# Turning the query tile of twenty middle token tiles with transposing transfers on SyncE's queue instead of fp16 transposes on TensorE

## The chip, the cores and the metric

The kernel runs on one core of a Trainium2 chip. Times are device microseconds (us) of one execution. The engines named here are TensorE (PE in the profile; PEld is its weight load, which overlaps it), VectorE (DVE), ScalarE (ACT), GpSimd (POOL) and SyncE (SP). SP computes nothing: it issues the DMA transfers, one after the other, in the order of its program. Each engine works through its own program strictly in order, and semaphores make one wait for another.

## The reference, cut to what matters

The input is 2048 tokens of 512 values. Four sublayers follow each other: Fourier mixing (A), a mixture of tiny experts (B), and both once more. Everything is computed in 32 bits, with a residual and a layer norm around each.

```python
def _A_ref(x, dft_seq_re, dft_seq_im, dft_hid_re, dft_hid_im):
    a = jnp.einsum("bsd,ed->bse", x, dft_hid_re)
    b = jnp.einsum("bsd,ed->bse", x, dft_hid_im)
    return jnp.einsum("ts,bse->bte", dft_seq_re, a) - jnp.einsum("ts,bse->bte", dft_seq_im, b)

def _B_ref(x, w_q, k1, k2, u, v):          # H = 32 heads, E = 16 keys a side, K = 2
    ...
    s1 = jnp.einsum("nhd,ed->nhe", q1, k1)
    s2 = jnp.einsum("nhd,ed->nhe", q2, k2)
    i1 = jnp.argsort(-s1, axis=-1)[..., :K]
    i2 = jnp.argsort(-s2, axis=-1)[..., :K]
    ...
    g = _softmax(top_s, axis=-1)          # top_s, top_e: the best 2 of the 4 sums, and their experts
    act = _gelu(jnp.einsum("nd,nhkd->nhk", xf, u[top_e]))
    return jnp.einsum("nhk,nhk,nhkd->nd", g, act, v[top_e])

x = x + _A_ref(_layernorm(x), ...)
x = x + _B_ref(_layernorm(x), ...)
x = x + _A_ref(_layernorm(x), ...)
x = x + _B_ref(_layernorm(x), ...)
```

## The kernel before

**Two layers of two stages.** Each layer (A and then B) is cut into nine units of the sequence: seven of 256 tokens and two of 128. For a unit, the sequence stage (`seq_unit`) multiplies the normalised input, kept whole in SBUF as a high part `xh`/`xg` and a low part `xl`/`xm`, by the columns of the sequence DFT. Those columns are streamed: a 256 KB piece is loaded into `raw` (line 454, four buffers), split by ACT into `ch` (line 458, three buffers) and by DVE into `cl` (line 462), and used by twelve matmuls of 512 columns (line 518), which add up in PSUM (`acc`). One piece is used up, and one is loaded, about every 2.7 us of pure sequence work.

**The token tiles.** When a unit is done, each of its tiles of 128 tokens goes through `token_tile`: the hidden DFT (line 668), residual, layer norm, a turn of the normalised tile, scores against the 2 x 16 keys of each of the 32 heads (lines 784 and 788), and products with the 256 experts (line 818). ACT evacuates the scores (line 793). DVE then searches the best two keys a side (lines 880 to 912) and builds `q`, three slices of 128 x 128 fp16: the first key's number, the second's, and the softmax weights. Line 985 writes the last of the keys and line 1007 the last of the weights. There are 32 tiles in all, 16 a layer.

**From `q` to the expert weights.** `q` has a token on each partition and must be turned. `f_pq` does it with three fp16 transposes on PE (line 1018), which read `q` as stationary operand and write the PSUM tile `pq`; it takes one of the four `bank` buffers for that. ACT copies `pq` to `qt` in another order of elements (`f_qt`, line 1022). DVE compares `qt` with a table of numbers (line 1041, four instructions of 1024 columns) and multiplies by the weights (line 1047, two), into `lr`. PE multiplies these in 32 small matmuls (`f_blocks`, line 1057), ACT evacuates them (line 1089), SP writes them to DRAM (line 1116, `gdr`) and reads them back in another order (line 1124, `gt`), and DVE multiplies the activations by them (line 1131). Most tiles of the second layer are put off after that: their last product is done at the end (`off`).

**What sets the order.** Every step is an `Op` of a planner (`Plan.run`) with an engine, a planned duration, the steps it waits for, and the buffers it takes and gives back. The planner simulates the engines by a list of costs and, at each point, takes for an engine the step that can start first, ties by priority. The instructions are then written out by planned start, so that each engine has one fixed order. A DMA step has a duration on SP, a `lag` until its data are there and a `shy` as margin. Work of the sequence stage has the lowest priority on PE: it fills the time in which tiles wait for other engines. While a tile is searched, PE works on the next unit's sequence stage, and DVE interleaves the search of one tile with the comparisons of another and with the `cl` of the pieces.

A third kind of transfer matters as a comparison: in most tiles the normalised tile is turned through DRAM. DVE turns its 32 x 32 blocks, SP writes them out (line 726, `xdr`) and reads them back in four transfers of 64 KB (line 735, `tok`).

Of the kernel before, what the change touches and what calls it, by code (L numbers as in the profile page):

```python
# [11 lines left out]
F16 = mybir.dt.float16  # L12
# [4 lines left out]
P = 128  # L17
# [7 lines left out]
SP = 1  # L25
# [13 lines left out]

def MOVED(layer, at):  # L40
    return at >= 2 if layer == 0 else at < NCH + NSC * (TPC - 1) - 2


def DEFERRED(layer, at):
# [33 lines left out]
class Plan:  # L78
# [10 lines left out]
    def op(self, engine, us, fn, after=(), take=(), last=(), prio=(0, 0), lag=0.0, behind=(), shy=0.0):  # L89
        o = Op(len(self.ops), engine, us, fn, [a for a in after if a is not None], list(take), list(last), prio, lag,  # L90
               list(behind), shy)
        for h in o.last:
            h.users += 1
        self.ops.append(o)
        return o
# [60 lines left out]
MM512, MM256, TR32, TR16, MMG = 0.230, 0.121, 0.110, 0.057, 0.026  # L156
# [6 lines left out]
def act(n):  # L163
    return 0.09 + n / 1.2e3
# [7 lines left out]
def spectral_peer_kernel(ctx: ExitStack, tc, x_in, cseq, ctile, dhid, wq, k1t, k2t, ut, vm, out):  # L172
    nc = tc.nc
# [6 lines left out]


    BUFS = {"acc": 4, "bank": 4, "raw": 4, "c": 3, "p": 1, "row": 4, "wr": 5, "wp": 2,
            "tok": 3, "sc": 1, "eq": 1, "act": 3, "q": 2, "top": 1, "qt": 1, "lr": 4, "gt": 1, "pp": 1, "gdr": 2, "xdr": 2, "bn": 1, "pick": 1}
    plan = Plan(BUFS)


# [41 lines left out]
    def work(shape, dtype, name, pool=None):  # L228
        return work_pool().tile(shape, dtype, name=name, bufs=BUFS[pool or name])
# [7 lines left out]
    op = plan.op  # L237
# [368 lines left out]
    last = {}  # L606
# [3 lines left out]
    def token_tile(layer, n, i, t0, at):  # L610

        prio = (0, layer, at if at < len(units) - 1 else -1 - layer, i)
# [5 lines left out]
        t = {}  # L618
# [6 lines left out]
        a = None  # L625
# [31 lines left out]
        for cs in wide:  # L657
            hb, nc_ = Hold("bank"), cs.stop - cs.start
            for z, (k, ms) in enumerate(steps):
                def f(z=z, k=k, ms=ms, cs=cs):  # L660
# [4 lines left out]
                    for c in range(2):  # L665
# [6 lines left out]
                a = op("PE", 2 * len(ms) * (MM512 if nc_ == D else MM256), f, [pready[layer, n][k][2 in ms], a] + dft_done + seed,  # L672
                       take=[hb] if z == 0 and not fine else [], behind=[a_row],
                       last=[phold[layer, n]] if z == len(steps) - 1 else [], prio=prio)
# [11 lines left out]
        if fine:  # L686
            a = ln_rest(lambda: t["bn"].rearrange("p a b -> p (a b)"), hbn, i, bn_done, prio)
        else:
            a = ln_stats(lambda: t["row"], i, [b] + ([xready[1, i]] if (1, i) in xready else []), prio)
# [60 lines left out]
        for z, k in enumerate([] if moved else ks):  # L750
# [16 lines left out]
            hb = Hold("bank")  # L767
            a = op("PE", (k.stop - k.start) * TR32, f_tr, [xn[z]], take=[hb], last=[hx], prio=prio)
# [7 lines left out]
        for hf in range(2):  # L776
            hb = Hold("bank")
# [21 lines left out]
            if fine:  # L799
                for z, k in enumerate(ks):  # L800
                    a_pe = op("PE", 2 * (k.stop - k.start) * MM512, lambda f=f_pch, hf=hf, k=k: f(hf, k), [a_th[z], a_pe],
                              take=[] if z else [hb], prio=prio)
# [8 lines left out]
        hb, hact, hg = Hold("bank"), Hold("act"), Hold("act")  # L811
# [13 lines left out]
        a = op("PE", 12 * MM256, f_xu, [a_pe], take=[hb], last=[hth, htl], prio=prio)  # L825
        a = op("ACT", act(N), f_act, [a], take=[hact], last=[hb], prio=late)
# [6 lines left out]
        a = op("ACT", act(N), f_g0, [a], take=[hg], prio=late)  # L833
        a = op("ACT", act(N), lambda: nc.scalar.activation(t["g0"], t["g0"], AF.Copy, bias=1.0), [a], prio=late)
        a = op("DVE", dve(N), lambda: nc.vector.tensor_mul(t["g0"], t["g0"], t["act"]), [a], prio=late)
        a = op("ACT", act(N), lambda: nc.scalar.activation(t["g0"], t["g0"], AF.Tanh, scale=C0), [a], prio=late)
        a = op("ACT", act(N), lambda: nc.scalar.activation(t["g0"], t["g0"], AF.Copy, bias=1.0), [a], prio=late)
# [3 lines left out]
        heq, hq, htop = Hold("eq"), Hold("q"), Hold("top")  # L841
# [91 lines left out]
        if fine:  # L933
            left, a_val, a_key, first = [], [], [], []
            for f in range(2):
                part = slice(f, f + 1), slice(f * H, (f + 1) * H), 32
                order_ = prio + (f,)
                a = largest(0, *part[1:], lambda f=f: t["pc", f], scored[f:f + 1], order_, **hold, behind=first)
# [5 lines left out]
                a = eq(0, *part[1:], view, a, order_)  # L944
                a = code(0, *part, a, order_)
                left += without(*part, view, a, order_, last=banks[f:f + 1], take=[] if f else [hsc])
                hold = {}
                a = tree32(1, *part[1:], left[f:], order_)
                a_val += a
                a = eq(1, *part[1:], lambda c=part[1]: flat("sc")[:, :, c], a, order_, last=[hsc])  # L950
                a_key += code(1, *part, a, order_)
        else:
            a = tree32(0, cols, w, sc_parts, prio, **hold)
            a = eq(0, cols, w, lambda: flat("sc"), a, prio)
            a = code(0, fs, cols, w, a, prio)
            a = without(fs, cols, w, lambda: flat("sc"), a, prio)
            a_val = tree32(1, cols, w, a, prio)
            a = eq(1, cols, w, lambda: flat("sc"), a_val, prio, last=[hsc])
# [48 lines left out]
        c5 = op("DVE", 0.13, lambda: nc.vector.tensor_sub(t["q"][:, 2, :, 1], t["gw"], t["q"][:, 2, :, 0]), [c4], last=[htop], prio=prio)  # L1007
# [14 lines left out]
            nc.scalar.copy(t["qt"].rearrange("p r (q j) -> p r q j", q=16),  # L1022
                           t["pq"].rearrange("p r (j q) -> p r q j", q=16))

        a = op("PE", 3 * TR16 + 0.06, f_pq, [c5, d2], take=[hb], last=[hq], prio=prio)
        a_qt = op("ACT", act(384), f_qt, [a], take=[hqt], last=[hb], prio=prio)

        def row_of(r, hf):
            m = t["qt"][:, r].rearrange("p (a b) -> p a b", b=4)[:, 16 * hf:16 * hf + 16]
# [79 lines left out]
        moves, back = [], []  # L1109
# [8 lines left out]
        for j in range(0 if fine else 2):  # L1118
            def f_in(j=j):
                if j == 0:  # L1120
                    t["gt"] = work([P, E, E], F32, "gt")
                d = t["gdr"][j]
                d = bass.AP(d.tensor, d.offset, [[STEP, 64], [4 * ROW, E], [1, E]])
                nc.sync.dma_start(t["gt"][j * 64:(j + 1) * 64], d)
# [220 lines left out]
```

## Time and profile before

| | us |
|---|---|
| median of 3 runs | 1233.59 (1233.14 to 1234.08) |
| the profiled execution, whole | 1233.48 |
| its span, first to last instruction | 1231.7 |
| DVE busy | 1000.1 |
| ACT busy | 492.2 |

Busy time is the time in which an engine runs at least one instruction. The instructions of PE overlap: a matmul of 512 columns is shown with some 390 ns, and the next one starts 0.23 us after it, so that what an instruction costs PE is the distance between two starts and not its duration. The same holds on DVE, where an instruction's shown duration reaches some 0.09 us into the next one.

### The profile page before, as it was taken

How to read it: one execution, taken by the hardware profiler on the slowest of the kernel's cores; microseconds unless marked ns; L12 is line 12 of the kernel's file. 1: busy time of each engine (PE TensorE's matmuls, PEld its weight loads, DVE VectorE, ACT ScalarE, POOL GpSimd, SP SyncE). 2: the span in 40 equal slices, each digit the busy share in tenths (PEclk: the TensorE clock that was granted, in tenths of full speed). 3: DMA queues.
4: the chain of work that ended last, by engine and by line, in shares of the span. 5: the costliest groups of instructions: out<-in, count | busy, mean ns of one | idle time of the engine just before them, and what ended most of it. 6: DMA issues, size and time to landing. Idle time of an engine off the chain costs nothing. (4 is left out here: it accounts for less than half of the span.)

```text
span 1231.7 us, 20733 instructions
## 1 busy us (share of the span) xinstructions
PE 1220.1 (99%) x7626; PEld 1014.5 (82%) x7626; DVE 1000.1 (81%) x2272; ACT 492.2 (40%) x1010; POOL 45.0 (4%) x71
## 2 busy tenths in 40 slices
PE   9999999999999999999999999999999999999998
PEld 6877778878788888899988988788888888888886
DVE  8899997999897785968987359959596786859796
ACT  7522234334343333324654233334343333343455
POOL 2000000000000000000000000000000000000000
PEclk9999999999999999999999999999999999999999
DMA  7866551453444244441656243563635254454464
GB/s 241 261 200 218 188 169 35 101 119 83 123 122 113 70 116 116 107 120 49 172 142 174 79 120 82 125 135 92 154 97 140 73 145 111 99 141 104 115 204 144
DMA packets 312726, 160.12 MB, mean 130 GB/s; under 512 B 216752, under 2 KB 283056, under 8 KB 312624
## 3 DMA queue, kind: packets, MB, share of 16 engines
q1 hardware_dynamic: 312480, 158.66, 48.2%
q8 instruction: 60, 0.98, 0.3%
q14 instruction: 42, 0.34, 0.1%
q10 hardware_dynamic: 144, 0.13, 0.0%
HBM read 120.73 MB, written 38.01 MB: 129 GB/s over the span
## 5 line engine op out<-in xcount | busy, mean ns | idle before, releaser
L518 PE MATMUL acc<-ch,xh 128*128 128x512 f32 (+1 forms) x868 | 328.3, 378 | 0.8 <-DVE ptl L547 0.8
L518 PE MATMUL acc<-cl,xh 128*128 128x512 f32 (+1 forms) x868 | 321.9, 371 | 0.0
L518 PE MATMUL acc<-ch,xl 128*128 128x512 f32 (+1 forms) x868 | 321.7, 371 | 0.0
L458 ACT CAST ch<-raw 128x512 fp32r<-128x512 f32 x256 | 158.6, 620 | 272.0 <-PE acc L518 222.7
L462 DVE TENSOR_TENSOR cl<-raw,ch 128x512 fp32r<-128x512 f32 x256 | 176.0, 688 | 61.6 <-ACT ch L458 51.4
L518 PEld LDWEIGHTS acc<-cl,xh 128*128 128x128 f32 x868 | 163.6, 188 | 28.8
L518 PEld LDWEIGHTS acc<-ch,xh 128*128 128x128 f32 x868 | 163.6, 189 | 28.0 <-issue 1.8
L518 PEld LDWEIGHTS acc<-ch,xl 128*128 128x128 f32 x868 | 163.8, 189 | 25.6
L880 DVE TENSOR_TENSOR tmp<-sc 128x512 f32<-128x512 f32 (+1 forms) x64 | 43.5, 680 | 72.9 <-ACT sc L793 72.6
L784 PE MATMUL bank<-wh,tok 128*128 128x512 f32 x256 | 100.3, 392 | 0.3 <-ACT tok L742 0.3
L784 PE MATMUL bank<-wl,tok 128*128 128x512 f32 x256 | 99.7, 389 | 0.0
L668 PE MATMUL bank<-dh,pth 128*128 128x512 f32 x248 | 98.6, 397 | 0.0
L668 PE MATMUL bank<-dl,pth 128*128 128x512 f32 x248 | 96.7, 390 | 0.0
L668 PE MATMUL bank<-dh,ptl 128*128 128x512 f32 x248 | 93.6, 390 | 0.0
L793 ACT COPY sc<-bank 128x512 f32<-128x512 f32 x62 | 36.1, 588 | 138.1 <-PE bank L788 108.0
L1041 DVE TENSOR_TENSOR lr<-iota,qt 128x1024 f16<-128x1024 f16 x124 | 81.0, 686 | 12.0 <-ACT qt L1022 11.9
L260 POOL TENSOR_TENSOR stats<-stats,half 128x1 f32<-128x1 f32 x64 | 43.7, 689 | 1149.1 <-DVE stats L257 1135.1
L867 DVE TENSOR_TENSOR eq<-sc,val 128x1024 f16<-128x1024 f32 (+1 forms) x64 | 77.2, 1207 | 1.5
L518 PE MATMUL acc<-ch,xg 128*128 128x512 f32 (+1 forms) x204 | 77.3, 379 | 0.0
L518 PE MATMUL acc<-cl,xg 128*128 128x512 f32 (+1 forms) x204 | 75.7, 371 | 0.0
L518 PE MATMUL acc<-ch,xm 128*128 128x512 f32 (+1 forms) x204 | 75.7, 371 | 0.0
L788 PE MATMUL bank<-wh,tok 128*128 128x512 f32 x256 | 68.4, 389 | 0.0
(190 smaller groups left out, 2057.8 us busy)
## 6 DMA issues: line engine op xcount, KB each, us to landing
raw<-in_cseq SPq DMA_DIRECT2D x224, 256.0 KB, 2.8
wr<-in_wq SPq DMA_DIRECT2D x32, 512.0 KB, 3.8
gdr<-lr SPq DMA_DIRECT2D x62, 256.0 KB, 3.7
raw<-in_ctile SPq DMA_DIRECT2D x32, 256.0 KB, 2.9
xdr<-lr SPq DMA_DIRECT2D x25, 256.0 KB, 2.8
tok<-xdr SPq DMA_DIRECT2D x100, 64.0 KB, 2.6
wr<-in_x SPq DMA_DIRECT2D x16, 256.0 KB, 3.3
row<-in_x SPq DMA_DIRECT2D x16, 256.0 KB, 4.0
```

Source lines behind the costliest of these rows:

```text
L260: nc.gpsimd.tensor_tensor(st[:, 1:2], st[:, 1:2], half, op=ALU.pow)
L458: nc.scalar.copy(t[1], t[0])
L462: nc.vector.tensor_sub(t[2], t[0], as32(t[1]))
L518: nc.tensor.matmul(target(d), w[s][:, d * P:(d + 1) * P], moving(s % per, part), start=(s == 0 and k == 0 and d % blocks == 0), stop=(s == ...
L668: nc.tensor.matmul(t["y", cs.start], w[:, k, c, t0:t0 + P], r[:, c, k, cs], start=(not fine and z == 0 and c == 0 and m == 0), stop=(z == ...
L784: nc.tensor.matmul(t["pc", hf], t["th"][:, k, :], r[:, k, hf], start=(k == 0 and r is wh), stop=False)
L788: nc.tensor.matmul(t["pc", hf], t["tl"][:, k, :], wh[:, k, hf], start=False, stop=(k == KD - 1))
L793: nc.scalar.copy(t["sc"][:, :, hf, :], t["pc", hf].rearrange("p h e -> p e h"))
L867: nc.vector.tensor_tensor(t["eq"][:, :, cols], scores(), val(rank_, cols), op=ALU.is_equal)
L880: nc.vector.tensor_max(t["tmp"][:, :, cols], flat("sc")[:, :8, cols], flat("sc")[:, 8:, cols])
L1041: nc.vector.tensor_tensor(t["m", hf, r], io2, row_of(r, hf), op=ALU.is_equal)
```

## The change

For the tiles of units 2 to 6 in the order of each layer (two tiles each, so ten tiles a layer and twenty in all), the three transposes on PE go. In their place SP issues three transfers with `transpose=True`, each of one 128 x 128 fp16 slice of `q`, from SBUF to SBUF, into a new buffer `qi`. The first two wait for the keys (`d2`), the third for the weights (`c5`). The ACT copy to `qt` stays and reads `qi` in place of the PSUM tile. The planner is given 0.5 us on SP for each, a lag of 3.0 and a margin of 0.5 us, and it makes a new order for all engines.

```diff
+def Q_MOVED(layer, at):
+    return 2 <= at < 7
...
-            "tok": 3, "sc": 1, "eq": 1, "act": 3, "q": 2, "top": 1, "qt": 1, "lr": 4, "gt": 1, "pp": 1, "gdr": 2, "xdr": 2, "bn": 1, "pick": 1}
+            "tok": 3, "sc": 1, "eq": 1, "act": 3, "q": 2, "top": 1, "qt": 1, "lr": 4, "gt": 1, "pp": 1, "gdr": 2, "xdr": 2, "qi": 1, "bn": 1, "pick": 1}
...
-        a = op("PE", 3 * TR16 + 0.06, f_pq, [c5, d2], take=[hb], last=[hq], prio=prio)
-        a_qt = op("ACT", act(384), f_qt, [a], take=[hqt], last=[hb], prio=prio)
+        if Q_MOVED(layer, at):
+            hqi, back = Hold("qi"), []
+            for r in range(3):
+                def f_in(r=r):
+                    if r == 0:
+                        t["pq"] = work([P, 3, P], F16, "qi")
+                    nc.sync.dma_start(t["pq"][:, r, :], t["q"][:, r].rearrange("p k a h -> p (k a h)"), transpose=True)
+                back.append(op("SP", 0.5, f_in, [(c5, d2)[r < 2]], behind=back[-1:], take=[] if r else [hqi], last=[hq], prio=prio, lag=3.0, shy=0.5))
+            a_qt = op("ACT", act(384) + 0.05, f_qt, back, take=[hqt], last=[hqi], prio=prio)
+        else:
+            a = op("PE", 3 * TR16 + 0.06, f_pq, [c5, d2], take=[hb], last=[hq], prio=prio)
+            a_qt = op("ACT", act(384), f_qt, [a], take=[hqt], last=[hb], prio=prio)
```

Three places of the new order follow, all around the first tile of the fifth unit of the first layer, a moved one. Line numbers of the change are 4 higher up to the diff's last piece and 14 higher behind it. The first place is PE, where this tile's products with the experts (line 818, in the change 822) end. Before:

```order
L818 MATMUL bank<-ul,tok 128x256
L818 MATMUL bank<-uh,tok 128x256
L1018 LDWEIGHTS q
L1018 MATMUL bank<-ident_109,q 128x128
L1018 LDWEIGHTS q
L1018 MATMUL bank<-ident_109,q 128x128
L1018 LDWEIGHTS q
L1018 MATMUL bank<-ident_109,q 128x128
L518 MATMUL acc<-ch,xh 128x512
L518 MATMUL acc<-ch,xl 128x512
```

And of the change:

```order
L822 MATMUL bank<-ul,tok 128x256
L822 MATMUL bank<-uh,tok 128x256
L522 MATMUL acc<-ch,xh 128x512
L522 MATMUL acc<-ch,xl 128x512
L522 MATMUL acc<-cl,xh 128x512
```

The transposes are gone. Between the last row of line 818 and the first of line 1057 (of the change, 822 and 1071) PE has 30 matmuls of 512 columns of the sequence stage before, and 45 in the change: the small products of this tile stand 15 matmuls later.

The second place is DVE, from the end of the same tile's `q` to its first comparisons with `qt` (line 1041, in the change 1055); `tmp`, `val` and `eq` belong to the search of the unit's other tile. Before:

```order
L985 TENSOR_TENSOR q<-key,df 128x2x64
L1007 TENSOR_TENSOR q<-gw,q 128x2x32
L880 TENSOR_TENSOR tmp<-sc 128x512
L887 TENSOR_TENSOR tmp<-tmp 128x256
L887 TENSOR_TENSOR tmp<-tmp 128x128
L887 TENSOR_TENSOR val<-tmp 128x64
L1041 TENSOR_TENSOR lr<-iota,qt 128x1024
L462 TENSOR_TENSOR cl<-raw,ch 128x512
L1041 TENSOR_TENSOR lr<-iota,qt 128x1024 x2
```

And of the change:

```order
L1011 TENSOR_TENSOR q<-gw,q 128x2x32
L884 TENSOR_TENSOR tmp<-sc 128x512
L891 TENSOR_TENSOR tmp<-tmp 128x256
L891 TENSOR_TENSOR tmp<-tmp 128x128
L891 TENSOR_TENSOR val<-tmp 128x64
L871 TENSOR_TENSOR eq<-sc,val 128x1024
L466 TENSOR_TENSOR cl<-raw,ch 128x512
L901 TENSOR_TENSOR eq<-eq,iota 128x1024
L839 TENSOR_TENSOR act<-act 128x256
L907 TENSOR_TENSOR eq<-eq 128x512
L466 TENSOR_TENSOR cl<-raw,ch 128x512
L1055 TENSOR_TENSOR lr<-iota,qt 128x1024 x3
```

Six instructions of the other tile and of the pieces have moved ahead of the first comparison.

The third place is SP, from the loads ahead of the same tile's three transfers to the transfers behind them. Before:

```order
L454 DMA raw<-in_cseq 128x2x256 x6
L1116 DMA gdr<-lr 128x8x64 x2
L622 DMA row<-in_x 128x512 x2
L454 DMA raw<-in_cseq 128x2x256
L1124 DMA gt<-gdr 64x16x16 x2
```

And of the change:

```order
L458 DMA raw<-in_cseq 128x2x256 x3
L1035 DMA_TRANSPOSE qi<-q 128x128 x3
L458 DMA raw<-in_cseq 128x2x256 x3
L626 DMA row<-in_x 128x512 x2
L458 DMA raw<-in_cseq 128x2x256
L1130 DMA gdr<-lr 128x8x64 x2
L458 DMA raw<-in_cseq 128x2x256
L1138 DMA gt<-gdr 64x16x16 x2
```

The three transfers stand in the middle of the loads of the sequence pieces, and three such loads are queued right behind them. Over the whole program SP has 60 of these rows, three for each of the twenty tiles.

## The prediction

> **What bounds the kernel now.** I read the page first: the engines' shares, and the clock that PE was granted.
>
> ```profile
> span 1231.7 us, 20733 instructions
> PE 1220.1 (99%) x7626; PEld 1014.5 (82%) x7626; DVE 1000.1 (81%) x2272; ACT 492.2 (40%) x1010; POOL 45.0 (4%) x71
> PEclk9999999999999999999999999999999999999999
> ```
>
> PE is busy for 1220.1 of 1231.7 us at an undisturbed clock. The time by stretches shows whether that holds where the change acts: the moved tiles of the two layers lie inside these two stretches. The columns are the stretch, its length, then busy time and instructions of PE, PEld, DVE, ACT and POOL, then clock, DMA share and GB/s.
>
> ```profile
> 250.00:620.00 370.00, 368.14 (x2233) 310.20 (x2232) 307.27 (x739) 144.22 (x303) 15.98 (x23) 1.00 0.44 110
> 790.00:1160.00 370.00, 369.18 (x2047) 305.18 (x2046) 278.92 (x642) 138.57 (x289) 6.47 (x12) 1.00 0.48 116
> ```
>
> In both, PE idles for under 2 us of 370, and ACT is busy for under 40%. The view of PE's waits (us in total, times, longest) says the same of the place of the change:
>
> ```profile
> PE bank L1162 <- DVE act L1131: 1.2, 2, 0.9
> PE bank L1057 <- ACT lr L1089: 0.7, 1, 0.7
> PE bank L1018 <- DVE q L985: 0.3, 1, 0.3
> ```
>
> So PE's stream of instructions sets the time. Work taken off PE is time gained one for one, as long as no new wait stands in that stream; and a wait in it is time lost one for one, since PE has no idle time in which to catch up.
>
> **What is removed.** The timeline of PE at the first moved tile of the fifth unit (start, duration, instruction):
>
> ```profile
> 428.16 0.28 PE L818 MATMUL bank<-uh,tok 128*128 128x256 f32 x1
> 428.28 0.34 PE L1018 MATMUL bank<-ident,q 128*128 128x128 f16 x3
> 428.43 0.47 PE L518 MATMUL acc<-ch,xh 128*128 128x512 f32 x1
> 428.74 0.39 PE L518 MATMUL acc<-ch,xl 128*128 128x512 f32 x1
> 428.97 0.40 PE L518 MATMUL acc<-cl,xh 128*128 128x512 f32 x1
> ```
>
> Starts count, not durations. From the first transpose to the second matmul behind them PE takes 428.74 - 428.28 = 0.46 us; one of the two steps is a matmul of 512 columns, which takes 428.97 - 428.74 = 0.23. The three transposes thus cost PE 0.23 us and not the 0.66 that three durations would give. Twenty tiles: 20 x 0.23 = **4.6 us**. The 0.3 us of the wait row above is too small to count. The PSUM buffer that is no longer taken releases nothing, since PE waits for no buffer worth naming.
>
> **What is added, and its cover.** Three transfers a tile stand between `q` and ACT's copy. The chain today, for the same tile, from the timelines of DVE, ACT and PE:
>
> ```profile
> 426.62 0.22 DVE L1007 TENSOR_TENSOR q<-gw,q 128x64 f16<-128x64 f32 x1
> 428.74 0.49 ACT L1022 COPY qt<-bank 128x384 f16<-128x384 f16 x1
> 429.32 0.69 DVE L1041 TENSOR_TENSOR lr<-iota,qt 128x1024 f16<-128x1024 f16 x1
> 433.53 0.69 DVE L1047 TENSOR_TENSOR lr<-lr,qt 128x1024 f16<-128x1024 f16 x1
> 435.45 0.69 PE L1057 MATMUL bank<-lr 128*64 128x64 f16 x32
> ```
>
> `q` is whole at 426.62 + 0.22 = 426.84, the copy begins 1.9 us later, DVE compares and multiplies until 434.22, and PE reaches its small products at 435.45, 1.2 us after they could begin. The change gives this chain more room on two engines. On PE the small products stand 15 matmuls later: 15 x 0.23 = 3.4 us, less the 0.23 that PE saves ahead of them, so 3.2. [...] On DVE six instructions stand ahead of the first comparison that stood behind it. Their groups (busy, mean ns of one):
>
> ```profile
> L867 DVE TENSOR_TENSOR eq<-sc,val 128x1024 f16<-128x1024 f32 x62 | 75.9, 1223 | 1.5
> L462 DVE TENSOR_TENSOR cl<-raw,ch 128x512 fp32r<-128x512 f32 x256 | 176.0, 688 | 61.6 <-ACT ch L458 51.4 <-PE acc L518 8.9 <-DMA xdr<-lr 0.9
> L897 DVE TENSOR_TENSOR eq<-eq,iota 128x1024 f16<-128x1024 f16 x62 | 42.5, 686 | 0.1
> L835 DVE TENSOR_TENSOR act<-act 128x256 f32<-128x256 f32 x32 | 13.5, 421 | 0.1
> L903 DVE TENSOR_TENSOR eq<-eq 128x512 f16<-128x512 f16 x62 | 26.2, 422 | 0.1
> ```
>
> With `cl` twice that is 1.22 + 2 x 0.69 + 0.69 + 0.42 + 0.42 = 4.1 us, or 3.6 by distances between starts (each shown duration reaches 0.09 us into the next). DVE thus comes to the comparison at 429.32 + 3.6 = 432.9; taking off the copy's 0.49 and 0.1 for handing over, the transfers must have landed by 432.3, **5.4 us after `q`**. Both engines give about the same room; I take 5.4.
>
> No row of before shows a transposing transfer, so its cost is bounded by other transfers. The plain load of a piece, the turn through DRAM and the reload of `gt`, from the views of their lines (min/median/max ns of the issue on SP), then us from issue to landing of the turn, and two rows of the page's list of issues (us to landing):
>
> ```profile
> L454 SPq DMA_DIRECT2D raw<-in_cseq x224: 367/373/1265, 1.2 to 1109.3; - x112
> L1124 SPq DMA_DIRECT2D gt<-gdr x62: 579/639/738, 226.4 to 1211.5; - x62
> L735 SPq DMA_DIRECT2D tok<-xdr x100: 562/628/845, 268.3 to 1101.6; - x100
> ...
> DMA to landing us min/median/max: 2.2/2.6/3.7
> x2d<-row SPq DMA_DIRECT2D x16, 256.0 KB, 2.0
> raw<-in_cseq SPq DMA_DIRECT2D x224, 256.0 KB, 2.8
> ```
>
> From below: an issue of 0.37 and a landing after 2.0, so the third slice is there 2 x 0.37 + 2.0 = 2.7 us after `q`. From above: the three run wholly one behind another, each as long as the slowest turn, 3 x 3.7 = 11.1 us. These ends are far apart on both sides of 5.4. The nearest row is the turn itself: it too comes in a row of small transfers that put data on other partitions. By it the third slice lands after 2 x 0.63 + 2.6 = **3.9 us**, and after 5.0 with the slowest landing seen. I take 3.9, which fits into 5.4 with 1.5 us to spare; PE then waits for nothing new.
>
> **The other queues.** SP gets 60 x 0.63 = 38 us of issuing, 1.9 us at a time, and in-order waits for `q`. Behind it stand loads of pieces. What they can bear is on the timeline of SP and ACT, and in the group of the cast:
>
> ```profile
> 430.63 0.37 SPq L454 DMA_DIRECT2D raw<-in_cseq  x1
> ...
> 431.93 0.62 ACT L458 CAST ch<-raw 128x512 fp32r<-128x512 f32 x1 [1.36 <-PE acc L518]
> 434.65 0.62 ACT L458 CAST ch<-raw 128x512 fp32r<-128x512 f32 x1 [2.10 <-PE acc L518]
> ...
> L458 ACT CAST ch<-raw 128x512 fp32r<-128x512 f32 x256 | 158.6, 620 | 272.0 <-PE acc L518 222.7 <-issue 21.3 <-PE bank L518 14.2
> ```
>
> Casts come every 2.7 us and wait for PE, not for a load. With four `raw` buffers, the piece issued at 430.63 is the fourth cast from 431.93 on, at about 431.93 + 3 x 2.72 = 440.1, while it lands in 2.8 (page). It can come some 6.7 us late before anything notices: 1.9 cost nothing, and 11.1 would. ACT, now waiting for a landing in order, has the next casts behind it. A cast may start up to two pieces' time less its own 0.62 and the 0.69 of `cl` late, some 4.1 us; on time as computed, it isn't late at all. The copy itself stays and now reads SBUF; whether it takes 0.4 or 0.6 there, ACT's idle time holds it.
>
> **The sum.** Profiled execution 1233.48 (span 1231.7 and 1.8 around it; 0.1 below the median of the runs) - 4.6 + 0 = **1228.9 us**. With the small unknowns (a new order may shift a wait or two, as the 1.2 and 0.7 us above) this case reaches from 1227.5 to 1231.
>
> **Rivals.**
>
> *Slower: the three transfers go one behind another.* If SP is held by each until it is nearly done, the third lands after 3 x 2.6 = 7.9 us, or 3 x 2.2 = 6.6 at the fastest landing, against 5.4. ACT's copy, DVE's comparisons and, in the end, the small products on PE (line 1057) are then 1.2 to 2.5 us late in each of the twenty tiles, and PE stops for it: 20 x 1.2 - 4.6 = +19, 20 x 2.5 - 4.6 = +45, so 1253 to 1279. It decides from 5.4 / 3 = 1.8 us of holding each. For it: nothing here has shown such a transfer, and the turn's issue (0.63) already costs more than the plain load's (0.37) though it moves a quarter of the bytes, so an issue is priced by pieces and not by bytes. Against it: no issue on SP has a median above 0.64 us in this trace. [...] Chance 0.36.
>
> *No change: SP's queue gives it back.* The three stand ahead of other tiles' stores and reloads (lines 1116 and 1124, three and five rows behind), and ACT and DVE wait for them in order. Today's reloads are waited for by DVE like this (us, times):
>
> ```profile
> DVE act L1131: 1.9, 2
> ```
>
> So they land just in time in the planned order. If 0.2 to 0.3 us of the 1.9 are passed on in each of the twenty tiles, 4 to 6 us are lost and the time is 1232.5 to 1235; with slightly longer issues up to 1240. It decides from about 0.23 us a tile. Against it: loads that wait for `cl` stand between, and give SP time to catch up. Chance 0.16.
>
> **How the numbers follow.** The forecast has 0.48, the slower rival 0.36, the queue 0.16, of which I count 0.10 within 0.2% (2.5 us, about what a measurement of this kernel can tell from no change) and 0.06 above it. So faster 0.48, same 0.10, slower 0.42. The forecast's own range is 1227.5 to 1231. The range for 8 in 10 must reach far into the slower rival: 1227.5 to 1275 leaves out some 0.04 below and 0.14 above.
>
> **What would show it.** On SP the issue of the new line at 0.4 to 0.7 us and a landing under 3.7 bear out the forecast; an issue above 1.8 is the rival. ACT's copy should begin within 5.4 us of line 1011's end (today 1007), DVE's first comparison should idle no more for it than now, and PE's wait at the small products should stay under 1 us in total. PE should have 60 matmuls less and its busy time some 4.6 us less. Waits of PE at line 1071, some 1 to 3 us each and twenty of them, would prove the forecast wrong, as would casts (line 458, now 462) that wait for loads.

## The result, and the profile after

| | before | change |
|---|---|---|
| median of five runs each (us) | 1234.08 (1233.14 to 1234.31) | 1238.24 (1237.86 to 1241.39) |
| ratio | | 1.0045, 95% interval 1.0034 to 1.0055 |
| the profiled execution (us) | 1233.48 | 1241.39 |

The change is slower by 0.45%, 4.2 us, where 4.9 us less were forecast. The five executions of the change lie in two groups, three at 1237.9 to 1238.2 with a mean granted clock of 0.998 to 0.999 and two at 1241.3 to 1241.4 with 0.997; the profiled one is of the second, so its times hold some 3 us more than the median, of which that difference of the clock, 0.001 to 0.002 of 1238 us, makes an estimated 1 to 2.5.

The page of the change, the same three rows as were shown of before:

```profile
span 1239.6 us, 20738 instructions
PE 1219.3 (98%) x7566; PEld 1014.2 (82%) x7566; DVE 1002.6 (81%) x2272; ACT 498.1 (40%) x1010; POOL 46.7 (4%) x71
PEclk9999999999999999999899999999999999999999
```

PE has its 60 matmuls less, but its busy time fell by 0.8 us only, and the span grew by 7.9. One slice of the clock, the twentieth, is no longer full. So PE stands still more than before, and in that slice it runs slower. The view of PE's waits (us in total, times, longest):

```profile
PE bank L672 <- ACT pth L548: 4.0, 2, 3.5
PE acc L522 <- DVE ptl L551: 3.2, 3, 1.4
...
PE bank L1022 <- DVE q L989: 1.2, 2, 0.9
...
PE acc L522 <- DVE xl L291: 0.8, 1, 0.8
PE bank L1071 <- ACT lr L1103: 0.7, 1, 0.7
...
PE bank L1071 <- DVE lr L1061: 0.3, 1, 0.3
```

The wait for `ptl` stood at 0.8 us in before and the one for `q` at 0.3; the first and the one for `xl` in the sequence stage were not among its ten longest. The small products (line 1071), where the slower rival would have shown up in twenty tiles, wait hardly more than before. What the new transfers cost is in the view of their line (issue on SP, min/median/max ns, and who waited), and what the copy costs in ACT's groups:

```profile
L1035 SPq DMA_TRANSPOSE qi<-q x60: 1103/1182/2082, 302.2 to 1154.7; - x60
...
  ACT qt L1026: 21.2, 12
...
DMA to landing us min/median/max: 2.2/2.3/4.6
```

```profile
L1026 ACT COPY qt<-qi 128x384 f16<-128x384 f16 x20 | 18.8, 940 | 21.2 <-DMA qi<-q 19.3 <-issue 1.9
L1026 ACT COPY qt<-bank 128x384 f16<-128x384 f16 x11 | 5.3, 478 | 5.5 <-PE bank L1022 5.5
```

An issue holds SP for 1.18 us, and a transfer lands 2.3 us after it began. Three in a row land 2 x 1.18 + 2.3 = 4.7 us after the first began, which stands about where `q` ends. The copy then takes 0.94 us, twice what the same copy takes from PSUM.

**Where the time went.** From the starts of the first matmul of the hidden DFT of four tiles (tile 4, tile 14, the first of the second layer, the last unit's) both traces can be cut into five stretches. Units are counted from 0 as in the diff, so the prediction's fifth unit is unit 4.

| us | start to tile 4 | tile 4 to 14 | change of layers | second layer | rest |
|---|---|---|---|---|---|
| moved tiles | 0 | 8 | 2 (unit 6) | 10 | 0 |
| before | 244.1 | 321.7 | 128.2 | 490.9 | 46.9 |
| forecast | 0 | -1.8 | -0.5 | -2.3 | 0 |
| change | +0.9 | +0.9 | +8.1 | -1.9 | -0.2 |

The second layer gains nearly what was forecast. In the eight tiles of the first layer 2.7 us are missing, and most of the loss is at the change of layers. The first stretch has the same order in all kernels; in the runs below it varies by -0.4 to +1.8 us, so that one profile tells a stretch to about a microsecond.

**The eight tiles: the end of unit 3.** The timelines of ACT, DVE and PE (start, duration, instruction, idle time before it and what ended that):

```profile
381.39 0.96 ACT L1026 COPY qt<-qi 128x384 f16<-128x384 f16 x1 [3.08 <-DMA qi<-q]
```

DVE in before, at the same tile:

```profile
377.88 1.90 DVE L1041 TENSOR_TENSOR lr<-iota,qt 128x1024 f16<-128x1024 f16 x3 [1.26 <-ACT qt L1022]
```

And in the change:

```profile
376.78 0.23 DVE L1011 TENSOR_TENSOR q<-gw,q 128x64 f16<-128x64 f32 x1 [0.27 <-ACT q L1010]
...
382.38 1.90 DVE L1055 TENSOR_TENSOR lr<-iota,qt 128x1024 f16<-128x1024 f16 x3 [3.62 <-ACT qt L1026]
384.20 0.68 DVE L1232 TENSOR_TENSOR row<-row,bank 128x512 f32<-128x512 f32 x1
384.80 0.68 DVE L466 TENSOR_TENSOR cl<-raw,ch 128x512 fp32r<-128x512 f32 x1
385.40 0.68 DVE L551 TENSOR_TENSOR ptl<-acc,pth 128x512 fp32r<-128x512 f32 x1
```

```profile
384.39 0.39 PE L522 MATMUL acc<-cl,xh 128*128 128x512 f32 x1
386.23 0.47 PE L522 MATMUL acc<-ch,xh 128*128 128x512 f32 x1 [1.45 <-DVE ptl L551]
```

`q` ends at 377.01, the copy begins 4.4 us later and ends at 382.35. DVE stands in order before its first comparison for 3.62 us, having nothing else to do ahead of it. In before it already waited 1.26 us for the copy at this place, and PE waited for nothing there. The work behind it is late too, up to `ptl`, the low part of the finished unit. `ptl` gives back PSUM buffers (`acc`) for which PE's next sequence matmul waits: 1.45 us of idle time. By starts that costs 386.23 - 384.39 - 0.23 = 1.61 us. The same chain at the end of unit 4 leaves PE idle for 0.94 us and costs 460.84 - 459.51 - 0.23 = 1.10. Together that is all of the 2.7 us.

**The change of layers.** SP, ACT and PE there:

```profile
597.55 0.33 SPq L1257 DMA_DIRECT2D raw<-x2d  x1
597.99 0.58 SPq L739 DMA_DIRECT2D tok<-xdr  x1
598.67 1.34 SPq L1138 DMA_DIRECT2D gt<-gdr  x2
600.06 1.86 SPq L739 DMA_DIRECT2D tok<-xdr  x2
601.97 0.63 SPq L626 DMA_DIRECT2D row<-in_x  x1
602.69 2.40 SPq L1035 DMA_TRANSPOSE qi<-q  x2
605.14 1.49 SPq L739 DMA_DIRECT2D tok<-xdr  x1
606.74 0.57 SPq L458 DMA_DIRECT2D raw<-in_cseq  x1
```

```profile
610.07 0.62 ACT L462 CAST ch<-raw 128x512 fp32r<-128x512 f32 x1 [3.67 <-DMA raw<-in_cseq]
610.59 0.58 ACT L548 CAST pth<-acc 128x512 fp32r<-128x512 f32 x1
```

```profile
607.33 0.39 PE L522 MATMUL acc<-cl,xh 128*128 128x512 f32 x1
611.22 0.80 PE L672 MATMUL bank<-dh,pth 128*128 128x512 f32 x1 [3.51 <-ACT pth L548]
611.82 0.63 PE L672 MATMUL bank<-dl,pth 128*128 128x512 f32 x1
612.24 0.63 PE L672 MATMUL bank<-dh,pth 128*128 128x512 f32 x1
```

SP issues without a pause from 597.55 to 607.31, and two of the transposing transfers stand in that row. The piece behind them is issued at 606.74, and ACT waits for it in order for 3.67 us. `pth`, next in ACT's order, needs nothing of that piece, but stands behind its cast, and PE waits 3.51 us for `pth`. After that the distance between two matmuls is 612.24 - 611.82 = 0.42 us in place of 0.23. The view by stretches of time (length, busy time and instructions of PE, PEld, DVE, ACT, POOL, then clock, DMA share, GB/s) shows why:

```profile
608.00:611.00 3.00, 0.00 (x0) 0.00 (x0) 0.28 (x1) 0.93 (x2) 0.00 (x0) 0.86 0.57 168
611.00:614.50 3.50, 3.28 (x8) 2.60 (x9) 3.50 (x7) 3.05 (x6) 0.00 (x0) 0.50 0.76 243
614.00:618.00 4.00, 4.00 (x13) 3.15 (x12) 1.76 (x4) 1.43 (x2) 0.00 (x0) 0.63 0.01 2
```

The clock fell to half during the wait: in shorter stretches it is 1.00 up to 610.0, 0.93 from there to 610.2, 0.50 from 610.2 to 617.0 and 1.00 behind that. It thus fell at about 610.2, some 2.4 us after PE's last matmul had ended (607.33 + 0.39). From 611 on it cost, as an estimate from these clocks, 3.5 x 0.50 + 4.0 x 0.37 = 3.2 us, less the half microsecond that is in both rows, so 3.0. In run 6 below it fell behind a wait of 1.50 us. Wait and clock make 6.5 of the 8.1 us; most of the rest are the waits for `q` (0.9) and for `xl` (0.8), both in this stretch. If the 3 us by which this execution is above the median lie here, as the clock suggests, an estimate for the median is 8.1 - 3 = 5 us.

### The profile page after: what moved, and what is told of

Same layout as the page of the kernel before. It is cut to its first block, busy times and chain, and to the rows that moved or that the text cites. A ratio compares the mean times of both kernels' runs of the same rounds, so it can differ in the third digit from the quotient of the medians.

```text
span 1239.6 us, 20738 instructions
## 1 busy us (share of the span) xinstructions
PE 1219.3 (98%) x7566; PEld 1014.2 (82%) x7566; DVE 1002.6 (81%) x2272; ACT 498.1 (40%) x1010; POOL 46.7 (4%) x71
```

## The experiments

The times measured are medians in us; "before" is the median of the runs of the kernel before on the same chip, ratios are with their 95% interval. The planner's costs, not only the range of tiles, are edited, since they decide the order. At the end a table has the stretches of all runs.

### 1. The planner is told the measured times

```diff
-op("SP", 0.5, f_in, ..., lag=3.0, shy=0.5)
+op("SP", 1.2, f_in, ..., lag=1.2, shy=0.5)
-a_qt = op("ACT", act(384) + 0.05, f_qt, back, ...)
+a_qt = op("ACT", act(384) + 0.55, f_qt, back, ...)
```

> The change with the planner told what the trace of the change shows: 1.2 us of SP for each transposing transfer, landing 1.2 us after that, and 0.5 us more for ACT's copy from SBUF (0.95 in place of 0.48). Theory (the transfers fit, but were planned with wrong shares, so that a few rows on DVE and one load on SP stand where they stop PE): the waits of PE at the ends of units 3 and 4 and the 3.7 us one at the end of unit 6 of layer 1 shrink to under 1 us together, time 1230 to 1232. Rival (SP and ACT cannot take this work wherever it is placed): still 1235 to 1241, with waits of several us at other places.

By these costs the third transfer is planned to land 3 x 1.2 + 1.2 = 4.8 us after the first begins, not 3 x 0.5 + 3.0 = 4.5; SP is taken for 2.1 us more a tile and ACT for 0.5.

Measured: 1231.90 against 1233.93, ratio 0.9986 (0.9977 to 0.9994). The same sixty transfers, in another order, make the kernel faster than before. The two waits for `ptl` and the 3.5 us are gone; one new wait stands at the change of layers, and the clock is low again behind it, 0.89 from 625 to 628 us and 0.66 from 628 to 632:

```profile
PE bank L788 <- ACT tok L746: 2.6, 1, 2.6
```

So the transfers as such don't cost the 4.2 us; their place in the order does. In the eight tiles it gains 3.3 us, more than the 1.8 of the forecast. Of the difference 0.9 is PE's wait for `act` there, 1.2 us in before and 0.3 in this order: a new order by itself moves a stretch by a microsecond or so. No run plans the kernel before anew with other costs, so how far its order could be bettered without any transfer is open.

### 2. Only the second layer

```diff
-    return 2 <= at < 7
+    return layer == 1 and 2 <= at < 7
```

> Transfers only in the second layer, ten tiles. Theory (the loss is made at three places of the first layer alone; the second layer gains its 10 x 0.23 = 2.3 us): 1231.5 to 1232.5. Rival (each moved tile costs about the same small amount): 10 tiles cost half of the change's +4.2, so about 1236.

Measured: 1234.35 against 1233.93, ratio 1.0001 (0.9992 to 1.0010), so neither of the two times that were expected. The second layer, which gained 1.9 us in the change, loses 0.9 here. PE's new waits are in it (0.8 of the first row stands in before too):

```profile
PE acc L522 <- DVE ptl L551: 1.8, 2, 1.0
PE bank L1071 <- DVE lr L1061: 1.1, 2, 1.0
```

The second layer was not a sure gain, either: its ten tiles have so little reserve that another order, made from the same costs, loses it.

### 3. Without the two tiles of the first layer's unit 6

```diff
-    return 2 <= at < 7
+    return 2 <= at < (7 if layer else 6)
```

> The change without the two tiles of unit 6 of the first layer, 18 tiles. Theory: the 3.7 us wait of PE for a piece's load at the end of that unit goes, and with it the stretch of 6.8 us at half clock where it follows; the waits at the ends of units 3 and 4 (1.6 and 1.1 us) stay: 1233 to 1235, and no execution near 1241. Rival (loss spread over the tiles): 1237.5 to 1238.

Measured: 1232.74 against 1233.93, ratio 0.9990 (0.9981 to 0.9999). The change of layers falls from +8.1 to +0.7 us: with these costs that stretch's loss hangs on the two tiles. The waits for `ptl` at the ends of units 3 and 4 are there in this order too, 1.2 us together in place of 2.4.

### 4. The transfers beside the transposes

The three transfers are issued into a tile that nothing reads, and PE's transposes stay.

```diff
-        t["pq"] = work([P, 3, P], F16, "qi")
-    nc.sync.dma_start(t["pq"][:, r, :], ..., transpose=True)
+        t["spare"] = work([P, 3, P], F16, "qi")
+    nc.sync.dma_start(t["spare"][:, r, :], ..., transpose=True)
...
-        else:
-            a = op("PE", 3 * TR16 + 0.06, f_pq, ...)
-            a_qt = op("ACT", act(384), f_qt, [a], ...)
+        a = op("PE", 3 * TR16 + 0.06, f_pq, ...)
+        a_qt = op("ACT", act(384), f_qt, [a], ...)
```

> The transposes stay on PE and feed ACT as before; the sixty transposing transfers are issued as well, into a tile that nothing reads. So SP and the DMA engines carry the whole load, and no chain waits for the transfers. Theory: PE's stream is as long as before and only the crowding of SP at the end of unit 6 can show, so 1234 to 1238, with waits of ACT's casts for loads of pieces there and none at the ends of units 3 and 4. Rival (the lateness of the copy alone costs, SP's queue nothing): 1234.0 to 1234.5. Rival (SP's holding costs everywhere): over 1238.

Measured: 1234.20 against 1233.93, ratio 1.0006 (0.9997 to 1.0015). Sixty transfers of the same length are there:

```profile
L1035 SPq DMA_TRANSPOSE qi<-q x60: 1102/1192/2129, 301.8 to 1146.7; - x60
```

They cost 0.3 us in the median, which the interval does not tell from nothing, and 1.1 at the change of layers in the profile. So what they load on SP and on the DMA engines is nearly hidden, in this order. Most of the loss arises where somebody waits for them.

### 5. The copy with its elements in the other order

The copy reads `qi` in a row and writes `qt` scattered, in the hope of a faster read.

```diff
+            if Q_MOVED(layer, at):
+                nc.scalar.copy(t["qt"].rearrange("p r (q j) -> p r j q", q=16),
+                               t["pq"].rearrange("p r (j q) -> p r j q", q=16))
+                return
```

> The change with one thing different: ACT's copy from SBUF reads the landed slices in their own order and writes in the scattered one, where the change reads scattered and writes in order. Every engine's order is that of the change. Theory (the chain from the end of q to qt is 4.7 us of transfers and 0.95 of copy, and late by about the 0.5 us that the copy takes longer): the copy takes about 0.5 us again, PE's waits at the ends of units 3 and 4 (1.6 and 1.1 us) shrink by 0.4 to 0.5 each, the wait at unit 6 stays: 1236 to 1237.5. Rival (the copy costs nothing, or is as slow in any order): 1238 to 1241 as the change.

Measured: 1255.60 against 1234.23, ratio 1.0173 (1.0159 to 1.0187). The edit did the opposite of what was meant; the planner didn't know of it, so that the order stayed the change's:

```profile
L1027 ACT COPY qt<-qi 128x384 f16<-128x384 f16 x20 | 38.6, 1930 | 21.4 <-DMA qi<-q 19.5 <-issue 1.9
```

Twenty copies, each 1930 - 940 = 0.99 us longer, cost (1255.60 - 1234.23) - (1238.24 - 1234.08) = 17.2 us, or 0.87 for each microsecond. These 17.2 us hold time lost to the clock too: its mean is 0.996 to 0.998 in the four executions, as against 0.997 to 0.999 in the change. In the change's order the chain from `q` to `qt` has, on average, hardly any reserve left; the prediction counted on 1.5 us of it.

### 6. The second layer alone, three transfers as one step

This keeps other tiles' stores from standing between the second and the third transfer, as they did at one tile of run 2.

```diff
-    return 2 <= at < 7
+    return layer == 1 and 2 <= at < 7
...
+            def f_in():
+                t["pq"] = work([P, 3, P], F16, "qi")
+                for r in range(3):
+                    nc.sync.dma_start(t["pq"][:, r, :], ..., transpose=True)
+            back = [op("SP", 1.5, f_in, [c5, d2], take=[hqi], ..., lag=3.0, shy=0.5)]
```

> Ten tiles of the second layer as in e2_second_layer, but the three transfers are one step of the planner, so nothing can stand between them on SP. Theory (in e2 the four stores of another tile, 3.3 us, stood between the second and the third transfer of one tile, which landed 8.2 us after q; that tile and the one behind it lost the 2.3 us that the layer should gain): no landing above 6 us after q, 1231.7 to 1232.8. Rival (the second layer cannot gain, since every tile's chain is late): 1234 as in e2.

Measured: 1235.70 against 1234.23, ratio 1.0012 (1.0003 to 1.0021). All landings are now within 5.6 us of `q`, and still the second layer loses 3.4 us in the profiled execution, which is 2.4 above the run's median. Its largest new wait, behind which the clock is 0.83 from 1090.5 to 1093.5 us and 0.66 from there to 1097:

```profile
1088.76 0.44 PE L1071 MATMUL bank<-lr 128*64 128x64 f16 x16
1090.69 0.44 PE L1071 MATMUL bank<-lr 128*64 128x64 f16 x16 [1.50 <-DVE lr L1061]
```

The stores in between were not run 2's cause. What is left is a chain of normal length in an order planned with a copy of half its time; what the planned costs do is told by run 14.

### 7. Runs 1 and 3 together: measured times, eighteen tiles

```diff
-    return 2 <= at < 7
+    return 2 <= at < (7 if layer else 6)
...
-op("SP", 0.5, f_in, ..., lag=3.0, shy=0.5)
+op("SP", 1.2, f_in, ..., lag=1.2, shy=0.5)
-a_qt = op("ACT", act(384) + 0.05, f_qt, back, ...)
+a_qt = op("ACT", act(384) + 0.55, f_qt, back, ...)
```

> e1_true_costs without the two tiles of unit 6 of the first layer, 18 tiles. Theory (e1 gains 4.6 us on PE and loses 2.7 us in one wait in the crowd behind unit 6, and more by the half clock after it): that wait goes, 1228.5 to 1230, which is the 18 x 0.23 = 4.1 us that the transposes took. Rival (the crowd on SP behind unit 6 is there without these two tiles): 1231.5 to 1232.5.

Measured: 1230.05 against 1234.23, ratio 0.9965 (0.9951 to 0.9979). This is the lowest median of all, 4.2 us below the kernel before; its interval overlaps with those of runs 10, 11 and 14. Eighteen tiles give up 18 x 0.23 = 4.1 us of PE. That the two agree is chance: the stretches with the moved tiles gain 3.3 and 2.8, and the change of layers, where none is moved now, loses 3.5.

### 8. A straight copy

The reordering of the tokens within a tile is left out: the copy is straight on both sides.

```diff
+            if Q_MOVED(layer, at):
+                nc.scalar.copy(t["qt"], t["pq"])
+                return
```

> The change with ACT's copy from SBUF done straight, both sides in order; the reordering of the tokens within a slice is left out for the twenty tiles, so what follows works on tokens in another order. All engines' orders are those of the change. Theory (the change's chain is late by the 0.47 us that the copy takes longer than planned; e5_copy_order, where it took 0.98 us longer still, lost 17.4 us, 0.89 us for each us and tile): the copy takes 0.4 to 0.5, the waits at the ends of units 3 and 4 fall below 0.6 each, 20 x 0.47 x 0.89 = 8.4 us less: 1229.5 to 1232. Rival (the transfers' 4.7 us and their hold of SP make the loss): 1237 to 1239.

Measured: 1237.33 against 1234.09, ratio 1.0024 (1.0015 to 1.0033). The copy is as short as it was from PSUM, and the largest wait is still there:

```profile
L1027 ACT COPY qt<-qi 128x384 f16<-128x384 f16 x20 | 10.2, 510 | 19.0 <-DMA qi<-q 19.0
```

```profile
PE bank L672 <- ACT pth L548: 3.6, 2, 3.2
```

This missed what was expected of it. Taking 0.43 us off each copy gains 2.1 us in the eight tiles and 0.6 in the second layer, but the change of layers stays at +7.1. The slow copy explains most of the loss at the ends of units 3 and 4; the wait on SP's queue at the change of layers has hardly anything to do with it.

### 9. Only the copy's time is told

```diff
-a_qt = op("ACT", act(384) + 0.05, f_qt, back, ...)
+a_qt = op("ACT", act(384) + 0.55, f_qt, back, ...)
```

> The change with the planner told 0.5 us more for the copy alone, the transfers planned as in the change (0.5 us of SP each). Theory (the copy's missing half us is what was planned wrong; the transfers' 4.7 us from the end of q to the last landing are inside the planned 5.0): most of e1's gain, 1231 to 1233. Rival (the SP times are what was planned wrong): 1236 to 1239.

Measured: 1236.84 against 1234.09, ratio 1.0020 (1.0011 to 1.0028). The copy's time alone does not give run 1's gain; run 12 tells the transfers' times alone.

### 10. Measured times, and the copy in two parts

The keys' two slices are copied after the second transfer and the weights' after the third; the comparisons wait for the first part only.

```diff
+            a_keys = op("ACT", act(256) + 0.35, f_part(slice(0, 2)), back[1:2], take=[hqt], ...)
+            a_qt = op("ACT", act(128) + 0.18, f_part(slice(2, 3)), [back[2], a_keys], last=[hqi], ...)
...
-    a = op("DVE", dve(1024, 2), f_m, [a_qt], ...)
+    a = op("DVE", dve(1024, 2), f_m, [a_keys], ...)
```

(with the times of run 1 on SP)

> e1_true_costs with the copy in two: the two slices of keys as soon as the second transfer has landed, the slice of weights behind the third, and DVE's comparisons wait for the first copy alone. The chain from q to the first comparison is some 1.5 us shorter. Theory (lateness of this chain is what costs): 1228.5 to 1231 with all twenty tiles; what is left is the crowd behind unit 6. Rival (e1's remaining loss is the crowd on SP alone): as e1, 1231.5 to 1232.5.

Measured: 1230.64 against 1234.09, ratio 0.9974 (0.9965 to 0.9983), with all twenty tiles. A shorter chain to the first comparison goes with half the loss at the change of layers, +2.1 in place of +4.8 in run 1.

### 11. Run 10 without unit 6

```diff
-    return 2 <= at < 7
+    return 2 <= at < (7 if layer else 6)
```

> e10_split_copy without the two tiles of unit 6 of the first layer. Theory: 1229 to 1230, as e7_true_costs_without_unit6 or a little under it, as nothing waits for the chain there either. If it is above e7 by over 1 us, more instructions on ACT cost something.

Measured: 1231.11 against 1234.09, ratio 0.9972 (0.9962 to 0.9982): not the 1229 to 1230 that was expected, and no better than run 10. It is 1.1 us above run 7, which the intervals do not tell from nothing. With the shorter chain the two tiles need not be left out.

### 12. Only SP's times are told

```diff
-op("SP", 0.5, f_in, ..., lag=3.0, shy=0.5)
+op("SP", 1.2, f_in, ..., lag=1.2, shy=0.5)
```

> The change with the planner told the transfers' measured times (1.2 us of SP each, landing 1.2 us after that), and the copy planned as in the change. Theory (what was planned wrong is SP: 1.5 us a tile where the transfers hold it for 3.6, so that what stands behind them on SP comes 2 us late): most of e1's gain, 1231 to 1233.5. Rival (both have to be told, or e1's gain is the luck of one order): 1235 to 1238.

Measured: 1235.92 against 1234.35, ratio 1.0016 (1.0007 to 1.0025). With runs 1 and 9 this makes a square, as differences to before: nothing told +4.2, the copy told +2.7, SP told +1.6, both told -2.0. Each alone gains 1.4 and 2.6, both 6.2. Neither of the two wrong costs is the cause alone. Whether they help each other (6.2 against 4.0) is hardly more than the intervals, some 1.1 us each, can tell.

### 13. Only the second tile of the first layer's unit 6 is left out

```diff
-        if Q_MOVED(layer, at):
+        if Q_MOVED(layer, at) and not (layer == 0 and i == 13):
```

> The change with the second tile of unit 6 of the first layer left on PE, nineteen tiles moved. Theory (this tile's chain makes ACT and DVE wait in the 80 us at the change of layers in which DVE has no reserve, 93% busy before, and PE loses 3.7 us and the half clock behind it there): 1233 to 1235, as e3 without both tiles of the unit (1232.7). Rival (the crowd on SP makes the loss, whatever this tile does): 1236.5 to 1239.

Measured: 1237.31 against 1234.35, ratio 1.0022 (1.0013 to 1.0030). This is the tile whose transfers stand ahead of the late piece. The wait of 3.5 us falls to 1.3, and the change of layers from +8.1 to +3.1 us, but the median gains only 1.2: the change's profiled execution stood 3.2 us above its median, this one 1.2 below. That tile alone is not the cause of the slowdown, as the rival expectation had it.

### 14. The second layer alone, with measured times

Run 2 with the costs of run 1.

```diff
-    return 2 <= at < 7
+    return layer == 1 and 2 <= at < 7
...
-op("SP", 0.5, f_in, ..., lag=3.0, shy=0.5)
+op("SP", 1.2, f_in, ..., lag=1.2, shy=0.5)
-a_qt = op("ACT", act(384) + 0.05, f_qt, back, ...)
+a_qt = op("ACT", act(384) + 0.55, f_qt, back, ...)
```

> Ten tiles of the second layer, as in e2, planned with the measured times of transfers and copy. Theory (the second layer gains its 10 x 0.23 = 2.3 us once the order has room for 4.7 us of transfers and 0.95 of copy): 1231 to 1232.5 where before is 1234.1. Rival (the second layer's tiles lose on their own what PE gains): 1233.5 to 1235.5 as e2 and e6.

Measured: 1231.27 against 1234.35, ratio 0.9974 (0.9964 to 0.9984). The second layer goes from +0.9 to -2.8 us by nothing but the costs, for ten tiles that free 2.3 us of PE by the forecast. PE's waits in that layer are those of before, 0.8 us for `ptl`. Here the forecast gain shows undisturbed.

### The stretches of all runs

Profiled executions, us, differences to before. A profiled execution lies within 1.4 us of its run's median, but for the change (3.2 above) and run 6 (2.4 above). PE's instructions in each stretch are the same in all kernels, apart from the transposes and, in some, three short matmuls that stand behind the mark of the last unit and not before it.

| run | start to tile 4 | tile 4 to 14 | change of layers | second layer | rest |
|---|---|---|---|---|---|
| the change | +0.9 | +0.9 | +8.1 | -1.9 | -0.2 |
| 1 measured times | -0.4 | -3.3 | +4.8 | -2.8 | -0.4 |
| 2 second layer | +0.1 | -0.1 | +0.4 | +0.9 | -0.2 |
| 3 without unit 6 | 0 | +0.4 | +0.7 | -1.9 | -0.1 |
| 4 both | +0.6 | -0.1 | +1.1 | -0.1 | -0.1 |
| 5 copy scattered | +0.8 | +8.9 | +6.9 | +7.0 | -0.2 |
| 6 one step, second layer | +0.6 | 0 | +1.0 | +3.4 | -0.4 |
| 7 = 1 and 3 | +0.4 | -3.3 | +3.5 | -2.8 | -0.4 |
| 8 straight copy | +0.1 | -1.2 | +7.1 | -2.5 | -0.1 |
| 9 copy told | +0.2 | -1.4 | +5.1 | -0.7 | +0.2 |
| 10 split copy | +0.2 | -2.7 | +2.1 | -2.2 | -0.3 |
| 11 = 10 and 3 | +1.8 | -2.7 | +1.8 | -2.2 | -0.3 |
| 12 SP told | +0.9 | -1.5 | +4.6 | -0.8 | -0.4 |
| 13 nineteen tiles | +1.0 | +0.3 | +3.1 | -2.0 | +0.1 |
| 14 = 1 and 2 | +0.3 | 0 | +0.8 | -2.8 | -0.4 |

## Why the prediction was wrong

**PE's gain: right.** 0.23 us a tile was forecast. Where the order fits, it is there: 2.8 us for the ten tiles of the second layer in runs 1, 7 and 14, or 0.28 a tile.

**The step that failed** is the room: "Both engines give about the same room; I take 5.4." It was worked out at one tile, the first of unit 4 (on DVE as 432.3 - 426.84, which is nearer to 5.5; on PE it is 1.9 + 3.2 = 5.1), and taken for all twenty. At that tile it holds: the copy begins 5.4 us after `q`, DVE waits 0.05 us for it, and PE not at all. But the prediction looked at no second tile of a unit. At those of units 3 and 4 DVE reaches the comparison soon after `q` (its last other work before the wait of 3.62 us is the product at 378.34), so most of the chain is a wait, and `ptl` stands behind it. In the new order DVE is free at 378.34 + 0.42 = 378.76; less the 0.59 for the copy and handing over, the transfers had to land 1.2 us after `q` (377.01), not 5.4. The trace of before had a sign of it: DVE waits for the copy there already, 1.26 us. The room is that of the tightest tile.

**Three terms of the chain were mis-sized, all to the same side.** The issue was taken as 0.63 us and is 1.18. The third landing was put 3.9 us after `q` and is at 4.7 (4.3 to 4.8 in sixteen of twenty tiles, 5.2 to 7.5 in the other four). The copy "takes 0.4 or 0.6 there, ACT's idle time holds it": it takes 0.94, and ACT's idle time doesn't hold it, since it lies on the chain between the landing and the comparison. From `q` to the comparison it is 4.7 + 0.94 + 0.1 = 5.7 us, where 5.4 + 0.49 + 0.1 = 6.0 was the room at the one tile looked at. So the reserve of 1.5 us was really 0.3 even there, and run 5 shows the same thing from the other side: a microsecond more costs 0.87.

**SP's queue: "1.9 cost nothing".** True over most of the kernel (run 4: 0.3 us in all), and wrong at the change of layers, where SP issues without a pause for 9.8 us. There 2.4 us of transfers stand ahead of a piece that comes late, and PE stops; without them (run 13) the wait is 1.3 us in place of 3.5. The reserve of 6.7 us for a piece had been read at unit 4 as well. The prediction had named casts that wait for loads as a sign against it, and they came (before, then the change; us, times, longest):

```profile
ACT ch L458 <- DMA raw<-in_cseq: 5.7, 4, 2.7
ACT ch L462 <- DMA raw<-in_cseq: 11.4, 7, 3.7
```

At the change of layers the kernel before is also tight on DVE, by the view of its stretches:

```profile
580.00:660.00 80.00, 79.66 (x539) 69.20 (x538) 74.16 (x182) 47.47 (x93) 3.01 (x4) 1.00 0.58 148
```

DVE is busy for 74.16 of 80 us here, 93%, against 307.27 of 370, 83%, in the first stretch that the prediction showed. That one ends at 620, in the middle of these 80 us, and averages them with quieter ones.

**The rivals.** The slower one (its 3 x 2.6 is 7.8 and not 7.9, which changes nothing here) didn't happen: an issue holds SP for 1.18 us and not 1.8 or more, and no wait of 1.2 to 2.5 us stands in each tile. The queue's time (1232.5 to 1240) was met, but by another mechanism than its own. SP's queue did give back a part, through a late piece at one place; the waits for reloads in every tile, by which the rival had it, are small. DVE's waits for `gt` rose from 1.9 us in 2 to this,

```profile
DVE act L1145 <- DMA gt<-gdr: 4.8, 10, 1.0
```

which is not where PE stops. That a few places decide, with waits of 1 to 3.5 us each, was in none of the cases.

**What stays open.** At the change of layers runs 1, 7, 9 and 12 lose 3.5 to 5.1 us, run 7 even with no moved tile there, while runs 2 to 4 and 14 lose 0.4 to 1.1. PE's waits in that stretch make the most of it: 0.3 us in before, 3.1 in runs 1 and 7, 4.0 in run 9 and 3.9 in run 12, and in run 1 the clock of 0.89 and 0.66 behind its wait besides. In runs 9 and 12 some 2.8 us of them, and in run 7 1.8, are waits for DVE. That fits a stretch without reserve on DVE, in which any disturbance of the order costs time, but why these orders disturb it is not shown. A busy DVE alone is not enough: from 300 to 380 it is busy for 72.92 of 80 us in before, and the change, whose first moved tiles lie there, takes 127.0 us from its tile 4 to the hidden DFT at 372.0 (before 127.2, to 371.3), so it loses nothing there.

## What to carry to other kernels

When a step off the bounding engine gets longer, add up its whole chain, each copy behind the transfer included, and set it against the room at the tightest place (second tiles, changes of phase, the stretch with the busiest second engine), not at one sample. In a kernel with a planned order, measure a new operation alone first and give the planner its real times: the same twenty tiles cost 4.2 us with the guessed ones and gained 2.0 with the measured. To tell a transfer's load from the wait for it, issue it beside the old path with nobody waiting.

## What the hardware showed that was not expected

- A transposing transfer of one 128 x 128 fp16 slice from SBUF to SBUF holds SP for 1.10 us at least and 1.18 in the median, nearly twice the 0.63 of a 64 KB load of the turn (line 735 of before), and lands after 2.3 us in the median, faster than that load's 2.6.
- ACT's copy of 384 fp16 elements a partition takes 0.48 us from PSUM with a scattered read, 0.94 from SBUF with the same read, 0.51 straight (run 8), and 1.93 with a scattered write (run 5).
- PE's clock fell to 0.50 within the wait of 3.51 us, and stayed there for 6.8 us. In run 6 it was still 1.00 from 1089 to 1090.5, nearly to the end of the wait of 1.50 us, and 0.83 from 1090.5 to 1093.5, with PE at work again from 1090.69; behind that the view by stretches has

```profile
1093.50:1097.00 3.50, 3.50 (x12) 2.79 (x11) 0.34 (x1) 0.30 (x2) 0.00 (x0) 0.66 1.08 243
```

  with a clock of 0.66. The wait of 1.45 us at the end of unit 3 was followed by a clock of 1.00 (383 to 393), and run 13, with one of 1.3, has a mean of 1.0 over its profiled execution. In the change the wait of 3.51 us cost its own length and, by the estimate above, 3.0 us more through the clock.
